# Folding a norm's factors into the weights of a fused linear-attention and gated-MLP kernel, with all f16 chunks on wide products

## The chip, the cores and the metric

The kernel runs on one core of one Trainium2 chip. The metric is the device time of one execution in microseconds (us): the median of three runs before the change is 502.85 us (502.32 to 502.93). One execution was also profiled. A chunk below is 128 time steps of one batch entry; there are 4 x 6 = 24 of them, numbered 0 to 23, and chunk c belongs to batch entry c mod 4.

## The reference

Two stages follow each other. The first is a linear attention with a decaying 48 x 48 state for each of 4 x 8 heads over 768 steps; the second normalises the 384 features of each of 3072 tokens and runs a gated MLP of width 1536.

```python
for t in range(S):                                   # S = 768, B = 4, H = 8, D = 48
    state = alpha[:, :, t, :, None] * state + einsum('bhd,bhe->bhde', k[:, :, t], v[:, :, t])
    y[:, :, t] = einsum('bhd,bhde->bhe', q[:, :, t], state)
x = y.transpose(0, 2, 1, 3).reshape(3072, 384)
rms = sqrt(mean(x * x, axis=-1) + 1e-06)
xn = x / rms * rms_g                                 # rms_g: 384 factors, one per feature
g, val = xn @ w_gate, xn @ w_val                     # 384 x 1536 each
out = (g / (1 + exp(-g)) * val) @ w_out              # 1536 x 384
```

## The kernel before, in words

All matrix products of weight run in f16. Each f32 operand is split into a high and a low f16 part, and a product is the sum of three: high x high, high x low, low x high (the list `SPLIT`).

**Attention, one chunk at a time** (`attention`, from L621). VectorE (DVE) scans the decays forward (L644), takes reciprocals (L664), scans backward, and multiplies k and q by the decays (L674, L681). ScalarE (ACT) rounds to f16 (`split_hi`, L496), DVE makes the low parts (L688, L715, L706). Chunks 0 to 3, the first of each batch entry, are done in f32 instead (L761, L788, L797, L807). For the others the state so far is decayed (gd at L722, sd at L733), split (ACT at L737, DVE at L741), and TensorE (PE) computes scores (L751) and the state's share of the output (L830) in one step. The scores are masked and split (L767, L878, L881) and multiplied by v (L851). `sums` (L924) adds the chunk's k-v product into two PSUM banks shared by an even and an odd chunk, and L934 and L940 add them to the state, chunk by chunk.

**Wide and narrow products.** L830 and L851 multiply one stationary operand with the high and the low part of the moving one. In a narrow chunk these are 24 products of 48 columns that add in PSUM. In a wide chunk (`WIDE`, chunks 10 to 23) the high and low parts are taken side by side: 8 products of 96 and 8 of 48 columns. The two halves of the result are then added by ACT (`take`, L868) and DVE (`add_up`, L872).

**Norm.** ACT sums the squares (L951, L953), GpSimd (POOL) raises the mean to the power -1/2 (L956), DVE multiplies the output by the 384 factors of `rms_g` (`gain`, L961; for chunks 0 to 3 both factors at once, L965), ACT and DVE split (L993, L996), and a transposing DMA or, for chunks 0 to 3, PE (L972, L986) puts the result into xT.

**Weights.** They arrive as 64-bit floats and are decoded into f32 by three instructions (L524 on ACT, L529 and L532 on DVE: "shift" and "join"), then split by ACT (`high`) and DVE (`low`, L540). For weight tile i0 alone the low part is made by PE (L549, L552) and ACT (L555).

**MLP.** `expert_in` (L1152) computes gate and value of one weight tile for a group of chunks in 18 products, ACT and DVE make h from them (L1163, L1169, L496, L1186); `expert_out` (L1471) and, for the last two groups, a scheme of seven instead of eight block products (L1353) form the output. Groups have 4, 2, 2, 4, 4, 4 and 4 chunks.

**What sets the order.** Each step is registered with a planner (`Plan.op`). Its order comes from the long table `ORDER`, a list of step numbers in base 36. `Plan.order` walks this list with the costs of `COST`, gives out buffers, and emits every engine's instructions in the order of the times that it works out. Where it finds PE idle in the first 45 us and a `mm` bank is free, it puts in filler products (`warm`, L1591) of 512 columns that nobody reads. Fourteen more stand at the very start (L605, on the tile `junk`).

Of the kernel before, what the change touches and what calls it, by code (L numbers as in the profile page):

```python
# [51 lines left out]
WIDE = range(10, 24)  # L52
# [11 lines left out]
    scan=1.2, rec=0.19, kh=0.605, qh=0.337, kl=0.6, vl=0.47, ql=0.6, gd=0.09, sd=0.28, sl=0.27, mask=0.6,  # L64
    al=0.6, st=0.31, ss=0.12, x=0.46, xl=0.53, shift=0.525, rest=0.88, wl=0.87, ob=0.46, oba=0.385,
    dec=0.11, k16=0.62, v16=0.515, q16=0.62, s16=0.26, a16=0.515, sq=0.7, x16=0.52, st0=0.23,
    abs=0.91, odd=0.47, cnt=0.85, wh=0.845, pow=0.6, sc=1.03, scw=0.955, sc32=0.6, yv=0.665, yvw=0.548, y32=1.4, add=0.47, take=0.4, u=0.82, po=1.48, xp=0.46, kp=0.5,
    neg=0.3, hs=1.47, hsh=1.05, hsl=1.2, tw=0.95, ts=1.2, th=0.74, tl=0.87, p7=0.75, snap=0.33, give=0.36, wid=0.75, wneg=0.22, wl2=0.37, rgw=0.7, rgt=0.37, x32=0.53, xb=0.38, ys32=0.82, kb=0.53, near=0.34, xneg=0.22,
# [23 lines left out]
6j a4 6n 46 2v e9 6r 6o 4f 47 6k al 6p 2w 6s 6t 2x 6q an 2q a6 6x jk 6u a8 am 6y ay az 6v ao 6z 3y 73 6w
b0 70 74 75 3z 71 40 79 4g 76 49 7a 72 7b aq 41 ar 7f ap aw 7c ew as 42 7g 7h 48 7d 7l 77 4h 7m 7n 78 7i
4a 4b 7r ax 7j at 7o bg 7s 4c 7p 7t 7k 4d 4l a5 4i 7x a7 7e 4j 4r 7q b1 7u 7y 7z 4e 7v e0 83 7w e2 4m 4n
4k 84 85 4o 4s 4t 53 89 a9 4p 86 4u 87 8a aa 8b 4x 4v 4q 80 8f 4w 81 54 ed 88 8c ab 8h 55 8g 8d 56 ac 82
59 57 4z 8l 4y ae ad 58 af 50 b2 8n av 51 5f 8m 8i ex b3 8j 52 5a 8k 8r b5 b4 b7 b6 5b 8s 8t 5c 5g 8o 5l
5d b8 bh 8u 8p b9 5h f7 5i 8x 8v ba e1 5r 5e 5j 8y e3 5m 8z e5 5n 5o 90 5k 5p 5x e4 5s 91 5q e7 5t 92 5u
8e 5v 93 f8 ag 5y 5z ah 94 5w 60 95 e8 61 8q ev 96 62 e6 8w 97 eb ib ic bi bb bk ee 98 bc ef ec bd eg ey
eh 9d 99 9e be 9f 9a f0 ei bf ez ek bj ej 9g im em 9b el f1 9c 9h f3 f2 9i ea f5 f4 id f9 kc bm kd 9j 9k
bn ie f6 bo if iq ig ft bs bt bp bu fb fc bq ii fd by br bv bl bw bz ih c0 ij ik c4 bx p5 in io en c5 p6  # L100
c6 c1 fa c2 fu c7 jb c8 ca fv cb jd cc jc jo jp fx jq cg il cd j8 ch je ci ce cm cf c9 c3 cn co fy fw ir
cs fe is ip eo cp jg cu ct jh cq er ep cr cy pg cv eq cj cw jf ff ck cx d0 lc es ke cz jm ji cl d4 kf et
kg kh d5 eu d6 da d1 d7 d2 ki d8 db dc fg kr dg fh fi fk fj dh di d9 dd dm fl de dj d3 dk jl fm dl ld ks
dn fn jj df kt k6 kj kn do kk fp fo q5 it ku fq le dp lf lg lh ds dq dr lr ls jr dt lt fr lu fs jn iu lj
lk li du kp iv sa kl iw ix dv km iy kq p7 fz dw dx p8 g0 p9 pa g1 g5 pc g2 g6 j0 g3 g7 iz gb pd g8 g4 j1
g9 pk ph gd gc j4 j2 q6 ga gh pb ge j3 x3 q7 js gf gj j5 gi gg lp ju q9 ll j6 gn q8 jw j7 qa go gp lm gt
gq gk gr gu jt gv gl gs jv gz qb gw jx h0 gx h1 gy qk k7 jy h2 jz ko qg lb k8 h3 h5 ka k0 kb k2 x4 h6 ln
k9 k1 mb pl h7 lo pm kv k3 h8 sb gm h9 k4 hb pi kw k5 pe ha hc pj hd ky qc hh qd he ra kx hi hf hj l0 kz
hn hk hg hl l1 ho hp pf l2 lq ht hq l3 hm hr l4 hu hv hs l5 ql h4 lv qm hw l6 l7 hx hz qn l8 lw qi lx ly
rc i0 qe lz m0 re i1 m1 l9 hy m2 la rd rf i2 m3 m4 mc rh i3 qf m5 i4 i5 md q4 sl m6 m7 xe pn mf m8 r4 i6  # L110
me qh m9 rb qj po ma ri mg i7 pp rn pq pr rg ps i8 pt rj w3 pu r5 xf i9 sc ia pv w4 mh rl r6 r8 pw r9 se
rk ro s9 mi mj r7 sd sf mn sh px sp sq py rp rq si sr mo q0 rr mp ss sg pz z8 w5 mt q1 mq w7 q2 mr mu w6
q3 w8 mv wa ms mz mw w9 mx rs my n0 n1 wi wj wb wk x5 13u qo n2 x7 n5 sn qp qq sj so qr qs n6 qt n7 qu
n3 sk n4 qv t9 n8 nb qw x6 we qx n9 mk qy na rt nd r0 ml nc wl ru qz wc rv rw mm r1 nh rx ne wg r2 nf wd
r3 ni wh nj ng rz rm nn nk z9 x8 nl no xa np xb nm x9 nt nq y8 sm nr ry y9 ns ta nv wf s0 tb x2 td nu te
s1 tc zj xi 13v xj s2 xk ya s3 nz yb s4 yc yd st o1 ye yf o0 xg sv nw xc sx xd nx o5 o2 y2 ny o3 s5 yn
o6 yo s6 xh o7 yg yp su 12v za ob sw zb zc o8 sy oc o9 o4 od oa sz y3 180 s7 176 t0 oe s8 oh y4 of zn zo
y5 yj og zp oi t1 yk t2 12w zd t3 oj 181 zf 182 183 ok zg ze t4 14t 12x on ol om 177 12z 12y oo 178 16x
130 t5 op yq t6 zq xl y6 y7 oq t7 184 t8 13a zk 185 wm 16u or ot 14u 13b zh wn os zl zi 13c ou wp 107
# [1648 lines left out]
```

## Time and profile before

| | |
|---|---|
| median of the runs | 502.85 us (502.32 to 502.93) |
| the profiled execution: its own time | 502.11 us |
| its span, first to last instruction | 500.3 us |
| PE busy | 492.7 us, 98% |
| DVE busy | 425.4 us, 85% |
| ACT busy | 283.5 us, 57% |
| POOL busy | 26.1 us, 5% |
| granted TensorE clock, mean | 1.000 |

The span is 1.8 us shorter than the time of the same execution. Busy is the union of an engine's instructions. A PE instruction counts from its issue to its modelled end, so neighbouring products overlap and a short pause between two of them can lie under the first one's end. Chip times are read as start to start where that matters.

### The profile page before, as it was taken

How to read it: one execution, taken by the hardware profiler on the slowest of the kernel's cores; microseconds unless marked ns; L12 is line 12 of the kernel's file. 1: busy time of each engine (PE TensorE's matmuls, PEld its weight loads, DVE VectorE, ACT ScalarE, POOL GpSimd, SP SyncE). 2: the span in 40 equal slices, each digit the busy share in tenths (PEclk: the TensorE clock that was granted, in tenths of full speed). 3: DMA queues.
4: the chain of work that ended last, by engine and by line, in shares of the span. 5: the costliest groups of instructions: out<-in, count | busy, mean ns of one | idle time of the engine just before them, and what ended most of it. 6: DMA issues, size and time to landing. Idle time of an engine off the chain costs nothing.

```text
span 500.3 us, 12723 instructions
## 1 busy us (share of the span) xinstructions
PE 492.7 (98%) x5210; PEld 312.0 (62%) x5210; DVE 425.4 (85%) x822; ACT 283.5 (57%) x751; POOL 26.1 (5%) x63
## 2 busy tenths in 40 slices
PE   8999999999999999999999999999999999999997
PEld 4678645568868876455465554456644469644497
DVE  7999999999999999999998899996599971276661
ACT  2779879556645765475655688755455641144420
POOL 4001000000010000000000000010000000000000
PEclk9999999999999999999999999999999999999999
DMA  8889565566553538523399976402100000100001
GB/s 321 330 269 241 182 217 171 173 167 193 100 130 120 116 91 165 132 84 118 107 278 258 353 233 231 143 1 65 48 1 16 18 0 18 47 2 0 1 10 60
DMA packets 47042, 65.22 MB, mean 130 GB/s; under 512 B 32641, under 2 KB 39042, under 8 KB 46978
## 3 DMA queue, kind: packets, MB, share of 16 engines
q1 hardware_dynamic: 46978, 64.36, 43.7%
q8 instruction: 41, 0.67, 0.6%
q14 instruction: 23, 0.19, 0.1%
HBM read 52.03 MB, written 4.72 MB: 113 GB/s over the span
## 4 chain that ended last, share of the span: by engine, by line
PE 83%; DVE 7%; issue 5%; DMA 3%; POOL 1%; ACT 1%; SPq 0%; POOLq 0%; DVEq 0%; ACTq 0%
PE mm L1152 52%; PE mm_po L1471 14%; PE mm_ab L1353 6%; PE at L751 3%; PE at_d L1353 2%; PE y L851 2%; DVE w L644 2%; DMA raw_c<-w_in 1%; DMA raw_o<-w_out 1%; PE at L924 1%; PE warm L1591 1%; PE y L830 1%; PE mm_warm L605 1%; POOL ss L956 1%; DVE h L1169 1%
## 5 line engine op out<-in xcount | busy, mean ns | idle before, releaser
L1152 PE MATMUL mm<-xT,wg 128*128 128x512 f16 (+1 forms) x1602 | 286.0, 338 | 0.5 <-DVE h L1169 0.4
L1152 PEld LDWEIGHTS <-wg 128*128 128x128 f16 x1602 | 154.6, 98 | 121.3 <-issue 0.9
L1471 PE MATMUL mm_po<-wo,h 128*128 128x384 f16 x576 | 96.9, 326 | 0.7 <-DVE wo L540 0.7
L496 ACT ACTIVATE h<-h 128x512 f16<-128x512 f32 (+1 forms) x89 | 46.0, 517 | 59.3 <-DVE h L1169 59.0
L1471 PEld LDWEIGHTS <-h 128*128 128x128 f16 x576 | 55.0, 98 | 36.4 <-issue 1.0
L1169 DVE SCALAR_TENSOR_TENSOR h<-mm,sl 128x512 f32<-128x512 f32 (+1 forms) x89 | 51.5, 582 | 14.5 <-PE mm L1152 14.2
L644 DVE TENSOR_TENSOR_SCAN w<-att,seed 112x520 f32<-112x520 f32 x48 | 59.5, 1239 | 2.5 <-DMA att<-att 1.8
L1163 ACT ACTIVATE sl<-mm 128x512 f32<-128x512 f32 (+1 forms) x89 | 45.2, 507 | 26.5 <-PE mm L1152 25.2
L1186 DVE TENSOR_TENSOR h<-h,h 128x512 f16<-128x512 f32 (+1 forms) x89 | 48.1, 546 | 4.3 <-ACT h L496 4.3
L956 POOL TENSOR_TENSOR ss<-ss,mhalf 128x1 f32<-128x1 f32 x24 | 20.1, 837 | 349.3 <-ACT ss L953 308.0
L767 DVE TENSOR_TENSOR at<-at,mask 128x512 f32<-128x512 f32 x40 | 26.8, 692 | 1.4 <-PE at L751 1.4
L881 DVE TENSOR_TENSOR a<-at,a 128x512 f16<-128x512 f32 x40 | 26.7, 682 | 0.0
L878 ACT CAST a<-at 128x512 f16<-128x512 f32 x40 | 22.8, 578 | 3.4 <-DVE at L767 3.2
L681 DVE TENSOR_TENSOR qp<-att,w 112x256 f32<-112x256 f32 x48 | 19.1, 420 | 0.3
L1353 PEld LDWEIGHTS <-h 128*128 128x128 f16 x216 | 17.8, 98 | 0.6
L751 PEld LDWEIGHTS <-k 48*128 48x128 f16 x480 | 13.4, 94 | 6.5 <-issue 6.5
L751 PE MATMUL at<-q,k 48*128 48x128 f16 x480 | 16.9, 217 | 0.0
L496 ACT ACTIVATE q<-qp 112x512 f16<-112x512 f32 x20 | 12.5, 624 | 7.8 <-PE y L830 6.1
L496 ACT ACTIVATION_READ_ACCUMULATOR h<-h 128x1 f32 x89 | 16.8, 189 | 0.0
L674 DVE TENSOR_TENSOR kh<-att,w 112x512 f32<-112x512 f32 x24 | 16.4, 685 | 0.1
L851 PEld LDWEIGHTS <-a 128*128 128x128 f16 x368 | 13.5, 96 | 3.0 <-DVE a L881 0.7
L851 PE MATMUL y<-v,a 128*128 128x96 f16 (+1 forms) x368 | 14.8, 190 | 0.6 <-DVE a L881 0.6
(200 smaller groups left out, 616.2 us busy)
## 6 DMA issues: line engine op xcount, KB each, us to landing
att<-att SPq DMA_DIRECT2D x22, 773.0 KB, 5.2
raw_c<-w_in SPq DMA_DIRECT2D x12, 768.0 KB, 4.6
raw_i<-w_in SPq DMA_DIRECT2D x11, 768.0 KB, 6.1
v<-vtok SPq DMA_DIRECT2D x24, 192.0 KB, 4.4
raw_d<-w_out SPq DMA_DIRECT2D x6, 768.0 KB, 5.4
out_dram<-ob SPq DMA_DIRECT2D x21, 192.0 KB, 2.7
raw_o<-w_out SPq DMA_DIRECT2D x5, 768.0 KB, 4.4
att<-att SPq DMA_DIRECT2D x2, 512.0 KB, 5.4
```

The costliest lines, as they stand in the source:

```text
L496: nc.scalar.activation(dst, src, AF.Copy, scale=scale, accum_out=stat[:rows, col : col + 1])
L644: nc.vector.tensor_tensor_scan(w, x, start.rearrange("r g p c -> r (g p c)"), 0.0, op0=ALU.mult, op1=ALU.add)
L751: nc.tensor.matmul(t["sc"][j][:, p, :], t["k16"][r, x, p, :], t["q16"][r, y, p, :], start=m == 0, stop=m == 2,)
L767: nc.vector.tensor_tensor(t["sc"][j], t["sc"][j], mask.to_broadcast([P, NP, C]), op=ALU.mult)
L851: nc.tensor.matmul(o, a_tile()[:, j, x, p, :], v, start=False, stop=p == NP - 1 and x == 1, skip_group_check=True,)
L881: nc.vector.tensor_tensor(a_tile()[:, j, 1], t["sc"][j], a_tile()[:, j, 0], op=ALU.subtract)
L1152: nc.tensor.matmul(ps[:, :n], wg[:, f, x, j, kk, :], xT[:, y, kk, cs], start=i == 0, stop=i == 3 * NK - 1,)
L1163: nc.scalar.activation(t["sl"][:, :n], t[0][:, :n], AF.Silu, scale=1.0 / (S_X * S_W))
L1169: nc.vector.scalar_tensor_tensor(t["h"][:, :n], t[1][:, :n], S_H / (S_X * S_W), t["sl"][:, :n], op0=ALU.mult, op1=ALU.mult,)
L1186: nc.vector.tensor_tensor(lo, used(t["h"][:, :n]), hi, op=ALU.subtract)
L1353: nc.tensor.matmul(bank(b), left(n, x, p), right(n, y, p), start=begin and p == 0 and m == 0, stop=end and p == n2 - 1 and m == 2, skip_gr ...
L1471: nc.tensor.matmul(t[i][:, :DM], h16_of(g, f)[:, x, ts], wo[:, f // 2, y, f % 2, :], start=f == 0 and m == 0, stop=f == NF - 1 and m == 2,)
```

## The change

Four things are edited at once. The table `ORDER` is new as a whole; of it only the first line is shown.

1. `rms_g` no longer multiplies x. It is loaded as a column of 3 x 128 values, scaled once by ACT, and multiplies the gate and value weights when they are split: `high` and `low` of the twelve i tiles run three times, over 256 of the 768 columns each, with one factor per partition. For tile i0, PE's `same` (a scaled unit matrix) becomes three matrices that carry the factors. `gain` is gone, and for chunks 0 to 3 the remaining multiplication moves from DVE to ACT. The PE product that spread `rms_g` over the partitions (L616) and its copy are gone.
2. `WIDE` begins at chunk 4: all f16 chunks are wide, six more than before.
3. The state of two batch entries lies in one tile. The decay, the split and the two additions run once for an even and an odd chunk, on 384 columns in place of 192. Scores of the even chunk come after the joined split.
4. `ORDER` holds another sequence, and `COST` new values for the changed steps.

```diff
-WIDE = range(10, 24)
+WIDE = range(4, 24)
-0 1 2 u 39 3 v 1k 4 7 w 2y 8 1l 9 a c d b h x 29 e i y z 10 3a 3b f g 3c j 11 3d 3f 12 17 13 k 3e l 9l
+0 1 2 u 3 v 39 1k w 7 4 2y 8 9 a b c h d x 29 e i f g y j 10 12 13 k 11 l 3a 3b 14 z m 3c n 17 15 3l o
...
         def high():
-            split_hi(dst[:, 0], t["uf"], col, S_W)
+            if not scaled:
+                split_hi(dst[:, 0], t["uf"], col, S_W)
+            for k in range(NK if scaled else 0):
+                split_hi(rows(dst[:, 0], k), rows(t["uf"], k), col + k, rg[:, k : k + 1])
...
+            for k in range(NK if scaled else 0):
+                nc.vector.scalar_tensor_tensor(
+                    rows(dst[:, 1], k), rows(t["uf"], k), rg[:, k : k + 1], rows(dst[:, 0], k),
+                    op0=ALU.mult, op1=ALU.subtract,
+                )
...
     def load_rg():
-        nc.sync.dma_start(rg[:1], rms_g.unsqueeze(0))
+        nc.sync.dma_start(rg, rms_col)
+
+    def rg_scale():
+        nc.scalar.activation(rg, rg, AF.Copy, scale=S_W)
 
     def rg_wide():
-        gains["w"] = buf(ps_mm, [P, 512], F32, "mm", "rg")[:, : DM]
-        nc.tensor.matmul(gains["w"], unit, rg[:1], start=True, stop=True)
+        for k in range(NK):
+            nc.scalar.activation(same[:, k], one, AF.Copy, scale=rg[:, k : k + 1])
...
-        def gain():
-            if cc not in WIDE:
-                t["x32"] = tl(ap, [P, DM], F32, "x32")
-            nc.vector.tensor_tensor(like(t["x32"]), y_sum(), like(rg), op=ALU.mult)
-
         def scaled():
             t["x32"] = tl(ap, [P, DM], F32, "x32")
-            nc.vector.scalar_tensor_tensor(
-                like(t["x32"]), y_sum(), t["ss"], like(rg), op0=ALU.mult, op1=ALU.mult
-            )
+            nc.scalar.activation(like(t["x32"]), y_sum(), AF.Copy, scale=t["ss"])
...
+        def s_decay():
+            nc.vector.tensor_tensor(S["sd"], S["st"], t["gd"].to_broadcast([R, 2, NP, D]), op=ALU.mult)
...
+        sd = add("DVE", "sd", s_decay, [gd] + [x[y] for x in was for y in ("st", "y")], [gd_k], lock=True)
+        sh = add("ACT", "s16", s_hi, [sd])
+        sl = add("DVE", "sl", s_lo, [sh], lock=True)
+        done = [x["rest"](sl) for x in both]
```

Three places show what the new order does. The first is VectorE near the start of the program: `a_1` is the masked score of chunk 1 (it releases PE's output step of that chunk), `w` the scan, `kh` and `qp` the products of k and q, `wu_i` a weight tile being decoded. Before:

```order
L674 TENSOR_TENSOR kh_284<-att_168,w_211 112x2x4x64
L681 TENSOR_TENSOR qp_289<-att_168,w_211 112x4x64 x2
L540 SCALAR_TENSOR_TENSOR wg<-wu_i_252,wg 128x768
L644 SCALAR_TENSOR_TENSOR w_322<-att_175,seed 112x520
L664 RECIPROCAL seed_98<-w_322 112x8
L644 SCALAR_TENSOR_TENSOR w_322<-att_175,seed_98 112x520
L777 TENSOR_TENSOR a_1_364<-at_0_329,near 128x256
L674 TENSOR_TENSOR kh_367<-att_175,w_322 112x2x4x64
L965 SCALAR_TENSOR_TENSOR x_0_370<-y_259,ss_362,rg 128x384
L777 TENSOR_TENSOR a_1_364<-at_1_330,near 128x256
```

And now, from the same product of chunk 1 on:

```order
L695 TENSOR_TENSOR qp_269<-att_169,w_207 112x4x64 x2
L688 TENSOR_TENSOR kh_277<-att_169,w_207 112x2x4x64
L523 TENSOR_SCALAR wu_i_296<-raw_i_174 128x768
L526 SCALAR_TENSOR_TENSOR wu_i_296<-raw_i_174,wu_i_296 128x768
L767 TENSOR_TENSOR a_1_327<-at_0_298,near 128x256
L767 TENSOR_TENSOR a_1_327<-at_1_299,near 128x256
L658 SCALAR_TENSOR_TENSOR w_345<-att_176,seed 112x520
```

The masked scores of chunk 1 now stand ahead of chunk 2's scans, and the low part of the first weight tile and the x of chunk 0 (`x_0`) no longer stand between.

The second place is ScalarE at the same point: `kT` is the transposed k of chunk 1, `ss` the norm of chunk 0, `sd` and `st` a state. Before:

```order
L903 ACTIVATE sd_298<-at_2_258 112x192
L895 ACTIVATE kT_320<-at_4_291,k_row 128x448
L906 ACTIVATE st_297<-at_2_258 112x192
L619 COPY rg<-mm_rg 128x384
L667 COPY dec<-w_322 112x8
L951 ACTIVATE junk,ssq<-y_259 128x384
L953 ACTIVATE ss_362<-ssq,eps 128x1
L524 ACTIVATE raw_i_182<-raw_i_182,t_add 128x768
```

And now:

```order
L893 ACTIVATE st_143<-at_2_242 112x192
L926 ACTIVATE junk,ssq<-y_243 128x384
L928 ACTIVATE ss_320<-ssq,eps 128x1
L885 ACTIVATE kT_340<-at_4_322,k_row 128x448
L935 ACTIVATE x_0_347<-y_243,ss_320 128x384
L629 ACTIVATE rg<-rg 128x3
L490 ACTIVATE wg,stat<-wu_i_296,rg 128x2x128 x3
L888 ACTIVATE sd_144<-at_2_352 112x192
```

x of chunk 0 now stands on ScalarE, behind the norm that POOL finishes and ahead of the first weight tile's three high parts and the state of chunk 1.

The third place is VectorE where the state is first decayed, for chunk 4 before (`sd_298`, 192 columns):

```order
L722 SCALAR_TENSOR_TENSOR gd_625<-dec 112x4
L777 TENSOR_TENSOR a_3_592<-at_1_552,near 128x256
L532 SCALAR_TENSOR_TENSOR wu_i_595<-raw_i_418,wu_i_595 128x768
L965 SCALAR_TENSOR_TENSOR x_2_644<-y_517,ss_610,rg 128x384
L1169 SCALAR_TENSOR_TENSOR h_0_0_0_659<-mm_0_0_1_615,sl_0_0_628 128x256
L733 TENSOR_TENSOR sd_298<-st_297,gd_625 112x192
```

And for chunks 4 and 5 together now:

```order
L658 SCALAR_TENSOR_TENSOR w_742<-att_578,seed_97 112x520
L1210 TENSOR_TENSOR h_0_3_819<-h_0_3_0_815,h_0_3_819 128x256
L1093 SCALAR_TENSOR_TENSOR gd_854<-dec 112x8
L695 TENSOR_TENSOR qp_856<-att_578,w_742 112x4x64
L1103 TENSOR_TENSOR sd_144<-st_143,gd_854 112x384
```

The joined decay stands behind chunk 5's backward scan (`w_742`), and the scores of chunk 4 come after it. On PE the filler of L1591, 39 products before, is 32 products now, and the scores of chunk 4, which stood behind the fourth weight tile's products, stand behind the first products of 512 columns (weight tile i5).

## Rows read from the trace of the kernel before

**Rows 1.** The page's busy times by engine, and the clock in 40 slices.

```profile
PE 492.7 (98%) x5210; PEld 312.0 (62%) x5210; DVE 425.4 (85%) x822; ACT 283.5 (57%) x751; POOL 26.1 (5%) x63
PEclk9999999999999999999999999999999999999999
```

**Rows 2.** Waits of PE: us in total, times, longest us.

```profile
PE mm_x L972 <- DVE x L965: 0.7, 1, 0.7
PE mm_po L1471 <- DVE wo L540: 0.7, 1, 0.7
PE y L851 <- DVE a L881: 0.6, 1, 0.6
PE mm L1152 <- DVE h L1169: 0.4, 1, 0.4
```

**Rows 3.** Busy us in one stretch: PE, PEld, DVE, ACT, POOL; clock, DMA share, GB/s.

```profile
100.00:150.00 50.00, 50.00 (x633) 38.34 (x631) 49.41 (x109) 27.69 (x88) 2.47 (x2) 1.00 0.62 148
```

**Rows 4.** PE in order of time: start us, us, what, count [idle before].

```profile
1.87 4.18 PE L605 MATMUL mm_warm<-junk 128*128 128x384 bf16 x14 [1.87 <-DVE seed L437]
5.89 2.54 PE L1591 MATMUL warm<-minus 128*128 128x512 f16 x11
...
9.37 2.76 PE L1591 MATMUL warm<-minus 128*128 128x512 f16 x12
...
15.09 0.91 PE L616 MATMUL mm_rg<-rg,junk 1*128 1x384 f32 x2
...
16.55 2.12 PE L1591 MATMUL warm<-minus 128*128 128x512 f16 x9
...
23.70 1.68 PE L1591 MATMUL warm<-minus 128*128 128x512 f16 x7
...
31.14 4.10 PE L1152 MATMUL mm<-xT,wg 128*128 128x256 f16 x36
```

**Rows 5.** The chain that ended last, four pieces: start us, us, what, count.

```profile
74.00 0.60 PE y L851 x24
...
79.26 0.30 PE y L830 x24
...
314.98 0.27 PE y L830 x16
...
330.90 0.54 PE y L851 x16
```

**Rows 6.** ScalarE in order of time, the last step ahead of the MLP: columns as in rows 4.

```profile
30.68 0.47 ACT L989 CAST xT<-mm_x 128x384 f16<-128x384 f32 x1
```

**Rows 7.** VectorE groups by line: count, busy us, mean ns, idle before.

```profile
L1169 DVE SCALAR_TENSOR_TENSOR h<-mm,sl 128x256 f32<-128x256 f32 x34 | 13.9, 416 | 0.0
...
L540 DVE SCALAR_TENSOR_TENSOR wg<-wu_i,wg 128x768 f16<-128x768 f32 x11 | 10.4, 951 | 0.0
L872 DVE TENSOR_TENSOR x<-y,x 128x384 f32<-128x384 f32 x14 | 7.7, 552 | 8.3 <-ACT x L868 8.2
L961 DVE TENSOR_TENSOR x<-x,rg 128x384 f32<-128x384 f32 x14 | 7.7, 552 | 1.4 <-ACT junk L951 1.4
...
L733 DVE TENSOR_TENSOR sd<-st,gd 112x192 f32<-112x192 f32 x20 | 7.1, 355 | 0.4
...
L965 DVE SCALAR_TENSOR_TENSOR x<-y,ss,rg 128x384 f32<-128x384 f32 x4 | 2.5, 614 | 0.1
```

**Rows 8.** ScalarE groups by line, in the same columns.

```profile
L496 ACT ACTIVATE h<-h 128x256 f16<-128x256 f32 x46 | 19.0, 413 | 26.2 <-DVE h L1169 26.1
...
L496 ACT ACTIVATE wg<-wu_i 128x768 f16<-128x768 f32 x12 | 10.1, 839 | 5.4 <-DVE wu_i L532 5.4
...
L496 ACT ACTIVATION_READ_ACCUMULATOR wg<-wu_i 128x1 f32 x12 | 2.3, 190 | 0.0
```

**Rows 9.** POOL's power of the norm, tile ss: ns min/median/max, and who waited.

```profile
L956 POOL TENSOR_TENSOR ss<-ss,mhalf x24: 549/603/2360, 17.5 to 386.4; 128x1 f32<-128x1 f32 x24
...
  ACT x L993: 1.9, 3
```

More of the change, by code (lines that the diff above doesn't have):

```diff
@@ L92 @@
[L92 to L96, printed above, removed]
@@ L144 @@
+1c8
 """
@@ L460, in tile_attn_moe @@
     nc.gpsimd.memset(minus, 0.0)
-    same = const.tile([P, P], F32, name="same")
+    same = const.tile([P, NK, P], F32, name="same")
     one = const.tile([P, P], F32, name="one")
-    nc.gpsimd.memset(same, 0.0)
     nc.gpsimd.memset(one, 0.0)
-    for x, value in ((minus, -1.0), (one, 1.0), (same, S_W)):
+    for x, value in ((minus, -1.0), (one, 1.0)):
         nc.gpsimd.affine_select(
@@ L563, in decode @@
             ps = [("at", (name, n)) for n in range(2)]
-            a = [add("PE", "wid", lambda n=n: bring(n), [o], [wu, ps[n]]) for n in range(2)]
-            o = add("ACT", "wh", high, [o], [wu])
+            a = [add("PE", "wid", lambda n=n: bring(n), [o, tiles["same"]], [wu, ps[n]]) for n in range(2)]
+            o = add("ACT", "wh3", high, [o, tiles["rg"]], [wu])
             a = [add("PE", "wneg", lambda n=n: less(n), [o, a[n]], [ps[n]]) for n in range(2)]
@@ L569, in decode @@
             return a[1]
+        if scaled:
+            o = add("ACT", "wh3", high, [o, tiles["rg"]], [wu])
+            return add("DVE", "wl3", low, [o], [wu], lock=True)
         o = add("ACT", "wh", high, [o], [wu])
@@ L1055, in attention, with meet, rest @@
             ql = add("DVE", "ql", q_lo, [qd], [key("qp"), key("q16")], lock=True)
-            gd = add("DVE", "gd", decay, [de, before["dec"]], [key("gd")])
-            sd = add("DVE", "sd", s_decay, [gd, before["st"], before["sl"], before["y"]], [key("gd")], lock=True)
-            sh = add("ACT", "s16", s_hi, [sd])
-            sl = add("DVE", "sl", s_lo, [sh], lock=True)
-            def meet():
-                scores()
-                from_state()
+            state_ops[cc] = dict(dec=de, s2=s2)
+        def meet():
+            scores()
+            from_state()
+        def rest(sl):
             ins = [key("k16"), key("q16"), at0, at1, key("y")]
             sc = ys = add("PE", "scw" if cc in WIDE else "sc", meet, [kl, ql, sl], ins)
-        if not first:
             m0 = add("DVE", "mask", lambda: masked(0), [sc], [at0])
@@ L1074, in attention @@
             y1 = add("PE", "yvw" if cc in WIDE else "yv", from_v, [l0, l1, vl, ys], ins)
-        y_k = key("y")
-        if cc in WIDE:
-            y_k = key("x32")
-            y1 = add("ACT", "take", take, [y1], [key("y"), y_k])
-            y1 = add("DVE", "add", add_up, [y1], [key("y"), y_k])
-        sq = add("ACT", "sq", square, [y1, tiles["rg"]], [y_k, key("ss")])
+            y_k = key("y")
+            if cc in WIDE:
+                y_k = key("x32")
+                y1 = add("ACT", "take", take, [y1], [key("y"), y_k])
+                y1 = add("DVE", "add", add_up, [y1], [key("y"), y_k])
+            sq = add("ACT", "sq", square, [y1], [y_k, key("ss")])
+            rt = add("POOL", "pow", root, [sq], [key("ss")], lock=True)
+            xd = add("ACT", "x16", x_hi, [y1, rt], [key("x32"), key("ss"), key("x16")])
+            xl = add("DVE", "xl", x_lo, [xd], [key("x32"), key("ss"), key("x16")], lock=True)
+            return sc, op("SP", 1.3, x_turn, [xl], [key("x16"), ("xT", g)], kb=300, kind="xt")
+        if not first:
+            kt = None if last else op("SP", 1.3, k_turn, [kl], [key("k16"), key("kT")], kb=300)
+            waiting[cc] = dict(de=de, rest=rest, sums=sums, deps=[kt, vl], use=[key("kT"), key("v16")])
+            if cc % 2:
+                xt_ops[cc - 1], xt = pair(cc - 1)
+                return xt
+            return None
+        y_k = key("y")
+        sq = add("ACT", "sq", square, [y1], [y_k, key("ss")])
         rt = add("POOL", "pow", root, [sq], [key("ss")], lock=True)
```

278 lines of the change are left out of this document (140 added, 138 removed).

## The prediction

> **What bounds the kernel now.** I read the busy times first. PE is busy for 492.7 of 500.3 us, DVE for 85%, ACT for 57% [rows 1]. A high share alone may be waiting in disguise, so the waits of PE came second: four of them, 2.4 us together [rows 2]. Third the stretches: between 100 and 150 us PE is busy for all 50.00 us and DVE for 49.41 [rows 3]. So PE sets the time, and DVE runs almost full beside it without making it wait; a microsecond saved on DVE or ACT is worth one only where PE waits for it. Fourth the start, where PE has nothing real to do for long: 1.87 us idle, 4.18 us of products on `junk`, and 39 filler products in four runs (11, 12, 9, 7), until the first product of the MLP at 31.14 us [rows 4]. From there it is real work to the end, with the waits of rows 2 between. The time is therefore the start's slack, plus PE's real work, plus few waits, and each part of the change is priced by what it does to these three.
>
> **The wide products.** Six chunks (4 to 9) change from narrow to wide. A narrow chunk's output step takes 0.60 us from its start to the next piece (x24), a wide one's 0.54 (x16); the state's share takes 0.30 and 0.27 [rows 5]. That is 0.06 + 0.03 = 0.09 us a chunk, 6 x 0.09 = 0.5 us less on PE, all on the path. The cost is one more pass of ACT and DVE over the output of these six chunks: on DVE 6 x 0.552 = 3.3 us [rows 7].
>
> **The start.** Three things go. The product that spread the factors is 0.91 us on PE [rows 4]. The fill: 39 products in 2.54 + 2.76 + 2.12 + 1.68 = 9.10 us are 0.233 us each [rows 4], and 32 remain, so 7 x 0.233 = 1.6 us less. The wait of 0.7 us for x of chunk 1 [rows 2] goes in its old form, since DVE no longer makes x; but I count nothing for it, because ACT makes it now and can be late just as well. Fill that is left out is a gain only if the real work then comes earlier. What DVE does ahead of chunk 3's q product, the last thing on it that PE needs before the MLP, shrinks by one join (a pass over 768 columns, as long as L540's 0.951 us) and by two x of 0.614 us, and grows by the split low part, 3 x 0.416 - 0.951 = 0.30 us: 0.95 + 1.23 - 0.30 = 1.9 us earlier [rows 7]. PE asks for 0.9 + 1.6 = 2.5 us. Both ends stay: 2.5 if ACT and PE were what the rest hung on, 1.9 if DVE was, and 0 if ACT, which takes over x, becomes late. I take 2.5, because what the first MLP product waited for last is on ACT: the rest of chunk 1's x, 0.47 us from 30.68 on, ends as that product starts [rows 6].
>
> **The weights.** The low part runs three times over 256 columns on DVE, 0.416 us each in place of 0.951: 11 tiles x 0.30 = 3.3 us more. I take L1169's mean, an instruction of the same kind and width that reads PSUM; the trace has none that reads SBUF alone at 256 columns. On ACT the high part was 0.839 + 0.190 = 1.03 us of entries and is now 3 x (0.413 + 0.189), about 1.8 (the second term from the same kind of accumulator read) [rows 8]: 12 x 0.8 = 9 us more. As parts overlap, this is the upper end; nothing is the lower. Tile i0's unit matrix in three parts multiplies the same 384 columns, so PE gains and loses nothing there; the bounds are 0 and 0.3 us for its four additional short products, and I take 0. What hides the work on ACT is its idle time, 43% of the span [rows 1]; that cover is thinnest in the first 50 us, where decoding and chunks 0 to 3 meet, and it is what the first two rivals are about.
>
> **Gain and state.** DVE loses 20 gains of 0.552 us, 11.0 us, and four x of 0.614, 2.5 us [rows 7]. Per pair of chunks the state's two decays and two splits on 192 columns become one each on 384, and so do the additions: 40 + 32 = 72 instructions of 0.355 us (L733 stands for all) become 36 of 0.552 (the length of L872, which has 384 columns): 25.6 - 19.9 = 5.7 us less. With the two additions from above DVE's sum is -11.0 - 2.5 - 5.7 + 3.3 + 3.3 = -12.6 us of 425. On PE's path this is worth nothing by itself [rows 1, 2]; at most it removes the three waits of rows 2 that do not belong to x, 0.7 + 0.6 + 0.4 = 1.7 us, and I keep that for the low end. What it adds is a wait: the even chunk's scores now need the odd chunk's backward scan too. Behind them on PE stand products of the MLP, and for the scores wait the mask and all that follows.
>
> **The sum** against the profiled execution: -0.5 - 0.9 - 1.6 = -3.0 us. Its span of 500.3 becomes 497.3, its time of 502.11 becomes 499.1. The median of the runs was 0.74 us above the profiled execution, so the prediction is 502.85 - 3.0 = 499.8 us.
>
> **Rivals.**
> *The norm's power holds up ACT.* POOL's power takes 0.603 us in the median and up to 2.360, and ACT waited for it three times, 1.9 us in all [rows 9]. Until now DVE itself stood waiting for that number in chunks 0 to 3; now ACT does, ahead of the high part of the first weight tile and the state of chunk 1, while DVE goes on with scans. If the power of one of these chunks takes the long value, ACT and then PE lose up to 2.36 - 0.60 = 1.8 us: -3.0 + 1.8 = -1.2, 501.6 us. Against it: the two lists leave ACT some slack there, and only the largest of 24 is known to be this long. [...]
>
> *The start's slack comes back as waits.* The products left out and the removed spreading of the factors are replaced by PE waiting for ACT's longer list. Then only the wide products count: -0.5, 502.3 us, no change. For it: DVE's share of the start shrinks by 1.9 us only, ACT's grows. Against it: PE's idle time in the old start was small beside its fill, so the order's allowances held there.
>
> *Slower: pairs.* The even chunk's scores wait for the odd chunk's scan, decay and split. If in each of the 10 pairs PE gets to them 0.45 us before the split state is there, 4.5 us come on top: -3.0 + 4.5 = +1.5, 504.4 us. It decides from 0.3 us a pair (3.0 us) on. For it: DVE has no spare time up to 150 us [rows 3], and in the first pair the joined decay stands directly behind the odd chunk's scan. Against it: 12.6 us less work on DVE is 1.3 us a pair, three times what would be needed.
>
> [...]
>
> That the change does not do what it says I give no case of its own: the counts of products are fixed, and a saving that fails to appear is the second rival.
>
> **How the numbers follow.** The forecast has 0.64; the power 0.13, the slack 0.11, the pairs 0.08, the clock 0.04. The forecast's own range is 498.2 (the 1.7 us of waits go too, nearly) to 501. A measurement of this kernel tells about 0.2%, 1.0 us, from no change; so faster is below 501.8 and slower above 503.9. Faster: nearly all of the forecast and of the power case, 0.77. Same: the slack case and a rest of the others, 0.12. Slower: 0.11. The range from 498.2 to 502.5 takes in the forecast, the power and the slack.
>
> **What would show it.** In the new profile, right: 32 fill products; the first MLP product some 2.5 to 3.5 us earlier than 31.14; output steps of chunks 4 to 9 with 16 products in 0.54 us; PE busy by about 3 us less with waits in all not above 3 us; DVE's busy time near 413. A step is wrong if the waits of PE name ACT in the first 45 us (slack, or, if ACT's wait names POOL's ss, the power), if they name DVE's state split L1109 at many pairs, or if the clock's row shows a digit below 9. The prediction fails as a whole if PE is no longer the engine that ends last, or if it waits for more than 5 us.

## The result and the profile after

The changed kernel takes 504.95 us (median of 7 runs, 503.65 to 505.87), the kernel before 502.19 (7 runs, 501.27 to 502.93): ratio 1.0052, 95% interval 1.0039 to 1.0065. It is slower by 2.8 us where 3.0 us less were forecast. The profiled execution took 503.93 us with a span of 502.2; against its fellow of before (502.11, span 500.3) that is 1.8 us more, and this is the difference that can be followed row by row. The first page of the profile after, the answer to [rows 1]:

```profile
PE 491.3 (98%) x5113; PEld 310.9 (62%) x5113; DVE 413.7 (82%) x779; ACT 288.6 (57%) x802; POOL 26.8 (5%) x61
PEclk9999999999999999999999999999999999999999
```

VectorE's work fell by 11.7 us, near the prediction's 12.6, and the clock held. PE's busy time fell by 1.4 us where about 3 were forecast. The start, in the columns of [rows 4]; the pieces of real work between are left out:

```profile
5.50 1.89 PE L1615 MATMUL warm<-minus 128*128 128x512 f16 x8
...
8.57 1.47 PE L1615 MATMUL warm<-minus 128*128 128x512 f16 x6
...
14.14 1.68 PE L1615 MATMUL warm<-minus 128*128 128x512 f16 x7
...
27.74 1.16 PE L1176 MATMUL mm<-xT,wg 128*128 128x256 f16 x9
...
41.44 0.55 PE L940 MATMUL mm_x<-one,x 128*128 128x128 f32 x3 [0.18 <-ACT x L935]
```

The fill is 32 products in seven runs (8, 6, 3, 7, 3, 2, 3), the spreading of the factors is gone, and the first product of the MLP starts 3.4 us sooner, 27.74 against 31.14 us. But at the end of the start, where chunk 3's x is turned, only a part of it is left. That place before:

```profile
42.83 0.55 PE L972 MATMUL mm_x<-one,x 128*128 128x128 f32 x3
```

42.83 - 41.44 = 1.4 us. The rest went into waits. PE's waits of the whole execution, the answer to [rows 2] (us in total, times, longest us; the wait for `junk` lies ahead of all work):

```profile
PE y L820 <- issue: 1.3, 1, 1.3
PE mm_warm L621 <- DVE junk L428: 1.2, 1, 1.2
PE mm L1176 <- DVE h L1193: 1.0, 2, 0.7
PE mm L1176 <- ACT sl L1187: 0.7, 2, 0.4
PE y L841 <- DVE a L871: 0.6, 1, 0.6
PE at_i L556 <- DVE wu_i L526: 0.5, 1, 0.5
PE at L878 <- DVE a L767: 0.4, 1, 0.4
PE mm_x L940 <- ACT x L935: 0.2, 1, 0.2
```

Without the second row that is 4.7 us, against 2.4 before and not above 3 forecast; the last row, ACT named within the first 45 us, is one of the prediction's own signs of a wrong step. The stretches show where (columns as in [rows 3]; before, 100 to 150 us had 50.00 of PE). First the kernel before from 50 to 100 us:

```profile
50.00:100.00 50.00, 49.35 (x453) 28.29 (x452) 49.01 (x80) 38.37 (x88) 1.92 (x2) 1.00 0.57 186
```

The kernel after:

```profile
50.00:100.00 50.00, 48.50 (x357) 26.62 (x355) 49.69 (x89) 42.73 (x119) 0.55 (x1) 1.00 0.66 194
100.00:150.00 50.00, 49.59 (x678) 38.01 (x677) 49.35 (x96) 28.93 (x95) 4.89 (x3) 1.00 0.51 139
150.00:200.00 50.00, 48.72 (x836) 38.80 (x834) 48.56 (x97) 30.30 (x97) 3.46 (x4) 1.00 0.47 115
```

VectorE is as full in the first 150 us as before: nearly all that it was spared (11.1 of 11.7 us) came behind 200 us. Behind 150 us PE waited for VectorE twice before (`h` 0.4 us at 165 us, `a` 0.6 at 275) and not at all now. The wide steps did their part; of the chain, chunk 4's output step answers to the first of [rows 5]:

```profile
71.17 0.54 PE y L841 x16
```

The start-to-start times of score, state and output steps add up to 1.68 us for a narrow chunk and 1.59 for a wide one, 0.09 us less as priced.

The last product of PE starts at 496.98 us before and at 497.40 after, 0.4 us later. The span grew by 1.9 us. So 1.5 us lie behind the last product, where the prediction had no term at all. The longest of SP's waits from 498 us on in the kernel after (SP issues the last stores and ends the program):

```profile
SPq L1787 <- DVEq L1701: 1.5, 1, 1.5
```

L1701 is the branch over the fallback code. VectorE passes it at 498.39 us and executes the next instruction at 501.19, 2.80 us later; before, the gap at the same place was 0.53 us, and the wait list has no such row. Within the gap the DMA record has a transfer of 8,192 bytes on an instruction queue, 499.36 to 499.88 us, 1.3 us ahead of VectorE's next instruction; the record does not name the engine that it is for.

The account of the profiled executions, forecast against outcome (us, on 502.11):

| | forecast | measured | missing |
|---|---|---|---|
| start, to chunk 3's x | -2.5 | -1.4 | 1.1 |
| from there to the last product | -0.5 | +1.8 | 2.3 |
| behind the last product | 0 | +1.5 | 1.5 |
| sum | -3.0 | +1.9 | 4.9 |

### The profile page after: what moved, and what is told of

It is laid out like the page before. It is cut to its first block, busy times and chain, and to the rows that moved or that the text cites. A ratio compares the mean times of both kernels' runs of the same rounds, so it can differ in the third digit from the quotient of the medians.

```text
span 502.2 us, 12490 instructions
## 1 busy us (share of the span) xinstructions
PE 491.3 (98%) x5113; PEld 310.9 (62%) x5113; DVE 413.7 (82%) x779; ACT 288.6 (57%) x802; POOL 26.8 (5%) x61
## 4 chain that ended last, share of the span: by engine, by line
PE 83%; DVE 8%; ACT 4%; issue 1%; DMA 1%; SPq 0%; DVEq 0%; ACTq 0%
PE mm L1176 49%; PE mm_po L1495 17%; PE mm_ab L1377 6%; PE at L741 3%; PE at_d L1377 2%; PE y L841 2%; DVE w L658 2%; ACT wg L490 1%; PE at L911 1%; DMA att<-att 1%; PE y L820 1%; ACT raw_i L518 1%; DVE wu_i L526 1%; DVE h L1193 1%; DVE qp L695 1%
## 5 line engine op out<-in xcount | busy, mean ns | idle before, releaser
L490 ACT ACTIVATE h<-h 128x256 f16<-128x256 f32 (+1 forms) x89 | 45.8, 515 | 20.3 <-DVE h L1193 20.2
L1210 DVE TENSOR_TENSOR h<-h,h 128x256 f16<-128x256 f32 (+1 forms) x89 | 47.6, 545 | 5.2 <-ACT h L490 5.1
L858 ACT COPY x<-y 128x384 f32<-128x384 f32 x20 | 9.5, 475 | 18.1 <-PE y L841 13.8
L490 ACT ACTIVATE wg<-wu_i,rg 128x256 f16<-128x256 f32 x36 | 17.9, 502 | 1.3 <-DVE wu_i L526 1.3
```

Of the source, the lines that this page charges most:

```text
L490: nc.scalar.activation(dst, src, AF.Copy, scale=scale, accum_out=stat[:rows, col : col + 1])
L1210: nc.vector.tensor_tensor(lo, used(t["h"][:, :n]), hi, op=ALU.subtract)
```

## The experiments

Theories: A, VectorE's code behind the branch has to be brought when it gets there, which depends on where the code lies. B, the 1.3 us at `y L820`, which the wait list gives to "issue" and not to another engine, are PE without code. C, the three-way split of the weights makes ScalarE and VectorE late in the first 130 us. Rivals: the joined state (for B), the end of a store (for A), the order itself (for C). Every ratio is to the kernel before on the same chip, whose median was 501.6 to 502.0 us in these comparisons.

### short_fallback and long_fallback_before: where VectorE's code lies

```diff
+    return                       # after: fallback code ends after its first half
...
+            for _ in range(96):      # before: 96 more in the fallback's loop
+                nc.vector.tensor_tensor(acc, acc, st, op=ALU.add)
```

> The kernel after, with the fallback code (which these inputs do not reach) cut to its first half; leaves out the second half of the fallback. All executed instructions are those of the kernel after. In the trace of the kernel after, VectorE's first instruction behind the branch over the fallback starts 2.8 us after the branch (501.19 against 498.39), in the trace of before 0.53 us after it, and SP's last wait is for that instruction. Theory A (VectorE's code behind the branch has to be fetched, because of where it lies): the gap falls to about 0.5 us, the end comes 1.5 us sooner with TensorE's last product at the same place, time about 503.4 us, ratio to before 1.002 to 1.003. Rival (the gap belongs to something else at the end, a store's completion or the semaphore itself): gap 2.8 us as before, ratio 1.005. Both: the wait of TensorE at y L820 (1.44 us near 170.7 us) is there again if it is a matter of the instruction stream.

Measured: gap behind the branch 0.52 us, last product to end 3.5 us instead of 4.8. SP's waits of the last microseconds no longer have VectorE's branch:

```profile
SPq L1789 <- PEq L1789: 0.8, 2, 0.6
SPq L1789 <- DMA out_dram<-x: 0.6, 1, 0.6
```

VectorE executed the same instructions (the other engines one to three fewer), so the 1.3 us are the place of the code; a store's end is not it. PE's wait at its output step was there again, as expected, with 0.9 us in the wait list (`y L822 <- issue`), 1.07 start to start. The time, 503.72 us, ratio 1.0047 (1.0028 to 1.0065), is lower than the changed kernel's but not by more than the intervals; TensorE's last product was 0.4 us later in this execution.

> The kernel before, with 96 VectorE additions added to the fallback code that is not reached. All executed instructions are those of the kernel before. Theory A: the gap behind VectorE's branch grows from 0.53 to about 2.8 us and the time by 1.5 to 2.3 us, to 503.7 to 504.5 us, ratio 1.003 to 1.0045. Rival: no change, 502.2 us, ratio 1.000.

Half a miss. The gap stayed at 0.51 us. But VectorE's last entry, the drain at the program's end, ran at 502.08 us, 1.1 us behind the last of the other engines, and a transfer on an instruction queue ended 1.4 us ahead of that: the last product to the end took 4.5 us instead of 3.3. Time 502.81 us, ratio 1.0017 (1.0007 to 1.0026), for 96 instructions that never run. The profiled execution was the slowest of twelve (504.13 us; its last product, too, came 1.0 us later than in the kernel before), so the cost of these instructions rests on the times and not on this profile. I read A as holding in kind, since that 1.1 us is again at VectorE's code and not at its work; which branch or end it hits I could not foretell. Over the thirteen traces of this study the gap is 0.5 us in eight and 2.8 to 3.4 in five, and the three kernels with the very same VectorE code (after, pe_code_shifted, high_one) all have 2.8 to 2.9.

### pe_code_shifted and v_load_later: TensorE's code

```diff
-        for _ in range(WARM_FIRST):
-            nc.tensor.matmul(ps[:, :DM], junk[:, :P], junk, start=True, stop=True)
+        for _ in range(46):
+            nc.tensor.matmul(ps[:, :117], junk[:, :P], junk[:, :117], start=True, stop=True)
```

> The kernel after, with the 14 fill products of 384 columns at the very start made 46 products of 117 columns: the same columns, 64 TensorE instructions more, so that all later TensorE code lies 64 instructions further on. Theory B (TensorE runs out of code near 170.7 us, where 457 of its instructions ran between two code transfers): the 1.44 us wait at y L820 goes or moves elsewhere, PE waits between 150 and 200 us fall from 1.4 to under 0.5 us, time 1.0 to 1.5 us less, about 503.7 us. Rival (the step waits for the joined state or for a bank): the wait stays at y L820 with 1.2 to 1.5 us, time 504.9 us.

The wait left `y L820` and stands, longer, in a product of the MLP just ahead of the scores:

```profile
PE mm L1176 <- issue: 2.0, 1, 2.0
```

In the kernel after, the trace has 4289 TensorE instructions (weight loads, products, nine semaphore instructions and a drain) ahead of the wait; in this one, with 64 more at the start, 4289 again, with other work at that place. In short_fallback, and in one_scale, low_one and high_one below, it is 4289 too. So in these six traces it is the count that decides and not the work. The page's row of one instruction queue (transfers, MB, share):

```profile
q8 instruction: 40, 0.66, 0.5%
```

Each of these 40 transfers has 16,384 bytes, and 10,248 TensorE instructions ran, 256.2 a transfer (in the kernel before 41 and 10,448, 254.8). That the queue is TensorE's is my reading of this count, as no record names the engine; so is, by theory B, that at the wait the next piece was not there. In the kernel after its transfer starts only as the last data of a batch come through (169.52 us, the data end at 169.76); it ends at 170.66, and PE goes on at 172.16. In the shifted kernel it starts at 168.47 with data on the queues until 172.0 us, and takes 2.70 us instead of 1.14. SP's issues ahead of that in the kernel after, and the DMA share (the last but one column):

```profile
160.29 1.23 SPq L706 DMA_TRANSPOSE kT<-k  x1
161.57 1.06 SPq L418 DMA_DIRECT2D v<-vtok  x2
162.72 0.38 SPq L413 DMA_DIRECT2D att<-att  x1
163.87 1.22 SPq L975 DMA_TRANSPOSE xT<-x  x1
```
```profile
165.00:169.50 4.50, 4.50 (x134) 3.92 (x131) 4.42 (x12) 3.12 (x12) 0.55 (x1) 1.00 1.05 191
169.50:172.00 2.50, 1.38 (x30) 1.02 (x28) 2.46 (x5) 0.90 (x5) 0.00 (x0) 1.00 0.04 9
```

Time 506.86 us, ratio 1.0095 (1.0078 to 1.0112): my 503.7 was wrong in sign, because the wait grew to 2.3 us start to start and the clock fell behind it:

```profile
174.00:176.00 2.00, 2.00 (x33) 1.57 (x28) 1.36 (x3) 1.29 (x3) 0.00 (x0) 0.50 0.00 0
```

PE had just stood for 2.3 us, up to 172.46 us, and the granted clock was 0.50 from 173.83 to 177.25 us, 3.4 us; behind the 1.4 us of the kernel after it stayed at 1.00.

v_load_later moves one step of the order, `v4` (v of chunk 16), behind `le`:

```diff
-... p2 l6 v4 jf l5 ...      ... ho le oz hp ...
+... p2 l6 jf l5 ...         ... ho le v4 oz hp ...
```

> The kernel after, with one load moved in SP's order: the 192 KB of v for chunk 16, issued at 161.6 us between four other transfers and not needed before 200 us, is issued about 20 us later. Theory B (TensorE's next code comes only when the transfers issued from 160.3 to 163.9 us are through; in the trace of the kernel after the code transfer starts at 169.52 us, when they end, and TensorE stands 1.44 us): the code transfer starts about 1 us sooner and the wait at y L820 falls from 1.3 to 0.3 to 0.6 us, time 0.8 to 1.0 us less. Rival (the wait belongs to the joined state or the y bank): the wait stays at 0.9 to 1.3 us.

The code transfer starts at 167.49 us instead of 169.52, again when the data end (167.7 us), and PE has no wait from 150 to 185 us. Chunk 11's score step starts 1.1 us sooner than in the kernel after, 180.96 against 182.03, and the last product at 496.30 against 497.40. That settles B against the joined state, which is untouched here. The time, 504.21 us, ratio 1.0050 (1.0036 to 1.0065), does not resolve it; the gap at VectorE's branch is still there, 2.98 us.

### one_scale, low_one, high_one: the split of the weights

```diff
-            for k in range(NK if scaled else 0):
-                split_hi(rows(dst[:, 0], k), rows(t["uf"], k), col + k, rg[:, k : k + 1])
+            split_hi(dst[:, 0], t["uf"], col, S_W)        # one_scale, high_one
...
-            for k in range(NK if scaled else 0):
-                nc.vector.scalar_tensor_tensor(rows(dst[:, 1], k), ..., rg[:, k : k + 1], ...)
+            nc.vector.scalar_tensor_tensor(dst[:, 1], t["uf"], S_W, dst[:, 0], ...)  # one_scale, low_one
```

> The kernel after, but each gate and value tile is split with one ScalarE and one VectorE instruction and the constant S_W, without the norm's factors, at the same places of the same order; it leaves the norm's factors out of the weights. Theory C (the three-way split makes ScalarE and VectorE late in the first 100 us): ScalarE busy falls by about 12 x 0.5 = 6 us and VectorE by 11 x 0.35 = 4 us; TensorE's waits between 28 and 42 us (2.2 us start to start) fall to about 1, those between 50 and 100 us (2.3 us) to under 1.5, time 1.5 to 2.5 us less, about 502.7 us. Rival (the order itself is what leaves the waits, the split does not matter): waits and time within 0.7 us of the kernel after.

> The kernel after, but VectorE makes the low halves of the gate and value tiles with one instruction per tile and the constant S_W instead of three with the norm's factors; ScalarE's three instructions per tile stay; leaves the factors out of the low halves. Theory C1 (VectorE's three-way low half, 1.2 us against 0.95, is what moves TensorE's start and the stretch to 130 us): the score step of chunk 7, at 131.4 us in the kernel after and at 129.5 in the one-scale kernel, starts at about 129.7; time 1.0 to 1.7 us under the kernel after. Rival C2 (it is ScalarE's list): it starts at 131.2 and the time is that of the kernel after within 0.5 us.

> The kernel after, but ScalarE makes the high halves of the gate and value tiles with one instruction per tile and the constant S_W instead of three with the norm's factors; VectorE's three per tile stay; leaves the factors out of the high halves. Theory C1 (VectorE): the score step of chunk 7 starts at 131.2 us, within 0.4 us of the kernel after, though ScalarE's busy time falls by 5 to 6 us. Rival C2 (ScalarE): it starts at about 129.7.

The score step of chunk 7 (the order is the same in all, so its start tells how late PE is by then) in the kernel after, one_scale, low_one and high_one:

```profile
131.38 0.84 PE L741 MATMUL at<-q,k 48*128 48x128 f16 x24
```
```profile
129.51 0.84 PE L740 MATMUL at<-q,k 48*128 48x128 f16 x24
```
```profile
131.32 0.84 PE L740 MATMUL at<-q,k 48*128 48x128 f16 x24
```
```profile
131.82 0.84 PE L741 MATMUL at<-q,k 48*128 48x128 f16 x24
```

Both halves together make PE 1.9 us late by 131 us. Kernels with the same weight work (pe_code_shifted, v_load_later, short_fallback) have this step at 131.5 to 131.9 us, up to 0.6 later than the kernel after; one_scale's 1.9 is clear of that, the differences of low_one and high_one are not. The time of one_scale is 501.97 us, ratio 0.9998 (0.9986 to 1.0010), 2.7 us less by the ratios. Half of that is the end (VectorE has 22 instructions less, its gap is 0.5 us, and last product to end takes 3.4 us instead of 4.8). The lead itself does not last: the last product comes at 496.89 us, 0.5 sooner, after PE lost 0.9 at 160 to 164 us to waits for `sl` and `h`, and 0.8 at 292 us, where VectorE waited 2.2 us for a transfer (`raw_c`). So C holds for the first 130 us. C1 and C2, one engine alone, did not come out as forecast; how the cost divides between the two engines stays open. In low_one PE is about 0.6 us ahead at 80 us and loses it at 101 us at a tile of `wo`:

```profile
PE mm_po L1494 <- DVE wo L540: 0.9, 1, 0.9
```

That wait is no mark of low_one: short_fallback and v_load_later have one for `wo` too, of 0.5 and 0.4 us, and the kernel before has one of 0.7. Its time, 502.28 us, ratio 1.0012 (1.0000 to 1.0023), is mostly the end again. high_one, 505.26 us, ratio 1.0078 (1.0060 to 1.0096), is no better than the kernel after. (one_scale and high_one also leave unused columns of ScalarE's sums, which GpSimd sets to a constant.) What the parts cost shows in the groups of the kernel after, which answer to [rows 7, 8] (count, busy us, mean ns, idle before):

```profile
L490 ACT ACTIVATE wg<-wu_i,rg 128x256 f16<-128x256 f32 x36 | 17.9, 502 | 1.3 <-DVE wu_i L526 1.3
L545 DVE SCALAR_TENSOR_TENSOR wg<-wu_i,rg,wg 128x256 f16<-128x256 f32 x33 | 14.0, 480 | 0.0
```

### code_moved: nothing but the place of the code

```diff
-        for _ in range(WARM_FIRST):         # 14 products of 384 columns
+        for _ in range(110):                # of 49 columns
...
+            if o["e"] == "DVE" and o["t"] > 400 and pads:   # 42 times
+                nc.vector.memset(spare, 0.0)
```

> The kernel after, with nothing changed but where code lies: the 14 fill products of 384 columns at the start are 110 of 49 columns (192 TensorE instructions more, so that the piece of code which ran out in the middle of chunk 9's score and output steps ends elsewhere), and VectorE gets 42 writes of one number after 400 us, where it is half idle, so that its branch lies at the place that it has in the kernel before. Theories A and B: no wait at y L820, the gap behind VectorE's branch 0.5 us instead of 2.8, the last product 1.0 to 1.4 us sooner and the end 2.5 to 2.9 us sooner: 502.1 to 502.5 us, ratio to before 1.000 to 1.001. Rivals: the wait at y L820 stays (504 us), or the gap stays (503.5 us), or another piece of code is late in its place.

The time is 502.91 us, ratio 1.0015 (1.0002 to 1.0028), clearly under the kernel after's, in the same order and with nothing more than 96 short products at the start and 42 small writes. In the profile the wait at the output step is gone and the gap at the branch is 0.53 us. But the profiled execution (504.40 us) was the second slowest of twelve, 1.5 us above their median, so it does not show where the median's gain lies. In it PE waits 2.0 us for `h` of VectorE instead of 1.0, and 0.9 us for ScalarE's `x` at chunk 1's output step (of this below, at the norm's power); the last product comes 0.5 us later than in the kernel after, and the end takes 4.7 us, because SP waits for a store:

```profile
SPq L1792 <- DMA out_dram<-x: 2.0, 2, 1.8
```

What made that store late stays open.

### searched_pad, searched_fallback, searched_flag_early: the order with the costs of the trace

```diff
-wh3=1.2, wl3=1.02, rgs=0.2, rgd=0.75
+wh3=1.46, wl3=1.21, rgs=0.2, rgd=0.9
-ORDER = """ ...                      # as shipped
+ORDER = """ ...                      # single moves, by the planner's own arithmetic
```

> The kernel after with the order searched again by single moves, with the costs that its trace shows for three steps (the high half of a gate and value tile 1.46 us where the planner had 1.2, the low half 1.21 for 1.02, the scaled unit matrices 0.9 for 0.75), and with orders left out in which 256 TensorE instructions in a row would pass while the transfers are full; 27 late one-number writes on VectorE put its branch where it lies in the kernel before. With these three costs the planner's arithmetic puts the end of the shipped order 2.2 us later than with its own, and its score steps then lie within 0.6 us of the trace; the searched order ends 1.35 us sooner than that. Theory (the order was set by costs that were too low, and code came late): TensorE's last product at 494.6 us (497.40 less 1.35 less 1.44 of the code wait), time 499.8 us if the end behind the last product takes 3.4 us and 501.2 if it takes 4.8; ratio to before 0.995 to 0.999. Rival (the waits of the first 130 us do not come from these costs): last product at 496 us or later, ratio 1.000 or above.

> The same searched order, without the 27 writes; instead nine kinds of VectorE instruction of the fallback code, which is not reached, are GpSimd's, so that VectorE's target behind the branch lies 12 instructions sooner. Last product at 494.6 us as in the other; the gap behind VectorE's branch is 0.5 or 2.8 us, by where the code lies, for which the runs so far give no rule; time 499.8 or 501.2 us.

> The order searched once more with the same three costs, and with the flag for the branch due 10 us before the end, since in the two searched kernels every engine reached the branch only behind 497 us (in the kernel after four of the five come to it before 497) and the end behind the last product grew from 4.8 to 6.2 us; 31 late one-number writes put VectorE's branch where it lies in the kernel before. Theory: last product at 496.0 us as in the searched kernel without code wait, end 3.4 us later, time 501.1 us, ratio to before 0.998 to 0.9995; if another engine's code is late at the end, 502.3. Rival (the late flag was not what lengthened the end): 6.2 us behind the last product, 504 us, ratio 1.0045.

With the three costs as measured, the planner's arithmetic puts the score steps of the shipped order at 55.8, 82.0, 131.4 and 157.7 us (chunks 4, 5, 7, 10), where the trace has 56.35, 81.90, 131.38 and 157.53; with the costs that the order was searched by they are 54.6, 79.8, 129.2 and 155.4. So the order was tuned on steps that take longer than it was told, by 2 us in all.

The first two searched kernels missed: 504.31 us, ratio 1.0048 (1.0034 to 1.0062), and 504.17, ratio 1.0046 (1.0033 to 1.0059). In searched_fallback the last product comes at 496.0 us, 1.4 sooner than in the kernel after, where 2.8 were expected: no wait of PE is given to "issue", but of the 1.35 us of the search nothing arrived, since PE waits for `wo`, `x` and `ob` at places that the planner has on time. The end grew to 6.2 us, as every engine now came to the branch behind 497 us, VectorE with a gap of 3.44 us there. searched_pad, in the profiled execution (507.16 us, the slowest of its six), lost 3.2 us more in the start, with a granted clock of 0.91 from 30 to 50 us:

```profile
30.00:50.00 20.00, 17.01 (x192) 13.77 (x191) 17.08 (x38) 16.76 (x58) 0.55 (x1) 0.91 0.70 252
```

searched_flag_early, with the flag due earlier and the order searched anew with it, has its last product at 495.49 us, 3.4 us of end, and 500.94 us (median of 11), ratio to before 0.9991 (0.9982 to 1.0000). That is 0.6% under the kernel after (1.0052) and level with the kernel before or a little under it; no other kernel here is faster by its median, and it leaves nothing of the reference out. That the early flag alone made the end short fits the 3.4 us against 6.2, but was not run by itself.

## Why the prediction was wrong

**Wide products: right.** -0.5 forecast, 0.09 us a chunk measured.

**Fill and spreading: right on their place, mis-sized at the end of the start.** This is the first step that failed. The step "PE asks for 2.5 us ... I take 2.5" measured 1.4 at chunk 3's x. The products left out came off in full (first MLP product 3.4 us sooner); the real work between 28 and 42 us then waited for VectorE's `h` (0.7 us), its `a` (0.4) and ScalarE's `x` (0.2). The bound 1.9 "if DVE was" and the rival "the start's slack comes back as waits" were the better reading, in part.

**The weights: the cost was right, the cover was wrong.** VectorE +3.3 us forecast, 14.0 against 10.4 measured, +3.6. ScalarE up to 9; its busy time is 288.6 us against 281.5 without the split, 7. The second step that failed is "what hides the work on ACT is its idle time, 43% of the span": all twelve tiles are decoded in the first 100 us, and from 50 to 100 us ScalarE is busy for 42.73 us (before 38.37) and VectorE for 49.69 (before 49.01). one_scale shows the price, 1.9 us by 131 us; of it 0.5 us is left at the last product. The share of the span said nothing on that stretch; the stretch's own row would have.

**Gain and state: right in size, worth little.** VectorE's sum fell by 11.7 us, nearly all behind 200 us. The prediction kept three waits, 1.7 us, for its low end; two of them, those behind 150 us (1.0 us in the wait list), are gone. Whether the spared work or the new order removed them is not shown.

**The pairs: right that they do not decide.** No row of waits names the joined split L1109. At the pairs' scores and outputs PE stood twice: for 1.4 us, by theory B for code, and for 0.6 us at chunk 5's output step for `a`, VectorE's low part of the masked scores; before, one output step waited 0.6 us for the same part.

**The clock: right.** Among the chances the clock has 0.04, for a slower kernel; in the kernel after, with 32 fill products, its row has no digit below 9. In the thirteen traces the granted clock fell ahead of the last product only in the two kernels in which PE stood for 2.3 us at once (pe_code_shifted, 0.50), or for 1.3 and 1.9 us closely behind each other (searched_pad, 0.91 from 30 to 50 us).

**The norm's power: the rival came true in other executions of this order.** POOL's instruction became longer:

```profile
L931 POOL TENSOR_TENSOR ss<-ss,mhalf x24: 549/734/2944, 14.5 to 398.0; 128x1 f32<-128x1 f32 x24
```

The median is 734 ns against 603, the longest 2944 against 2360 [rows 9]. Why is not shown. In the profiled execution of the kernel after, ScalarE waited for POOL in no row of the first 45 us. There POOL's first power began 0.24 us ahead of VectorE's scan:

```profile
14.53 0.56 POOL L931 TENSOR_TENSOR ss<-ss,mhalf 128x1 f32<-128x1 f32 x1 [8.41 <-ACT ss L928]
14.77 1.23 DVE L658 TENSOR_TENSOR_SCAN w<-att,seed 112x520 f32<-112x520 f32 x1
```

In high_one, the same order, it began 0.07 us behind the scan's start, and ended 0.36 us behind its end:

```profile
14.73 1.23 DVE L658 TENSOR_TENSOR_SCAN w<-att,seed 112x520 f32<-112x520 f32 x1
14.80 1.52 POOL L931 TENSOR_TENSOR ss<-ss,mhalf 128x1 f32<-128x1 f32 x1 [8.66 <-ACT ss L928]
```
```profile
ACT x L935 <- POOL ss L931: 1.1, 1, 1.1
```

That is the rival's chain, and in code_moved it is the same: PE stood for 1.3 us at chunk 1's output step. By chunk 4's scores nothing of it is left in high_one and 0.6 us in code_moved. The rival's aside that VectorE stood waiting for that number in the kernel before is in no row of its first 45 us.

**What had no term.** This is the third step that failed, and the largest: the sum puts all time in which PE waits for no engine, and all time behind the last product, at nothing. The runs show 1.4 us in which PE waited for no engine, by theory B for code (the shift and the moved load speak for it), and 1.5 us more behind the last product, of which VectorE's branch makes 1.3 (A, shown by short_fallback). Together they are 2.9 of the 4.9 us missing. The start and its waits are 1.1. The other 0.9 is a difference of two. Counted start to start, where the next product comes 0.15 us or more later than is usual (the median) behind one of that width, PE lost 3.2 us from 42 to 150 us, against 1.1 before; behind 150 us, without the wait for code, it lost 0.5 against 1.9. So 2.1 us came on and 1.4 went, which is 0.7 of the 0.9. Of the start's 1.1 and these 2.1, one_scale removes 1.9 by 131 us. That the order had been searched on costs too low fits these waits, but a search on better costs gained less than its arithmetic said, so it is not shown to be the whole of it. The medians differ by 0.9 us more than the two profiled executions do (2.8 against 1.8). The long power of high_one and code_moved, which the profiled execution of the kernel after did not meet, is a candidate; that it is the reason is not shown.

## What to carry to other kernels

Ask of the stretch in which added work falls, not of the span, whether the engine has room; relief for an engine counts only in the stretch where someone waits for it. This kernel, 98% full, was also tuned to where its code lies (0.5 or 2.8 us at VectorE's branch) and when its transfers end (a wait of 1.4 us, or none with one load moved): a wait that the profile gives to "issue", and time behind the last product, want an experiment that moves code alone before any story on the data flow. When costs in a planner are estimates, measure the new steps first and search after.

## What the runs showed of the hardware

In the kernel after one instruction queue carried 40 transfers of 16,384 bytes while 10,248 TensorE instructions ran, 256.2 a transfer; in the kernel before 41 for 10,448. That these are TensorE's code is my reading of the count. In six of the thirteen traces (after, short_fallback, pe_code_shifted, one_scale, low_one, high_one) PE stood after the same 4289 instructions, for 0.85 to 2.3 us, waiting for no engine. In five of these the transfer on that queue began 0.25 us before a batch of data transfers was through (169.52 us against 169.76 in the kernel after), and with a load moved away it began sooner, again 0.25 us before the data's end (v_load_later, 167.49 against 167.74), and PE did not wait; in pe_code_shifted it began with data still on the queues and took 2.70 us instead of 1.14. In all six PE went on 1.3 to 1.5 us after the transfer had ended. Behind its branch over code that is not run VectorE's next instruction came after 0.5 us in eight traces and after 2.8 to 3.4 in five; short_fallback (0.52 against 2.80) shows that the place of the code alone can make this difference here, and 96 instructions that never run made the kernel before 0.17% slower (long_fallback_before). What decides on the place stays open. After a stand of 2.3 us the granted clock was 0.50 for 3.4 us (pe_code_shifted); after one of 1.4 us it stayed at 1.00 (after). A GpSimd power of one column that began 0.24 us ahead of VectorE's scan took 0.56 us (after); one that began 0.07 us behind the scan's start took 1.52 and ended 0.36 us after it (high_one).
